# An attention and feed-forward kernel on one core: bits of the second head pair scaled in halves, four small transfers on ScalarE's queue, and several steps placed earlier in the order of units

## The chip, the cores and the metric

The kernel runs on one core of a Trainium2 chip. The metric is the device time of one execution in microseconds (us); the kernel before took 973.36 us, the median of 3 runs (972.34 to 974.44). A core has TensorE (PE, with its weight loads shown as PEld), VectorE (DVE), ScalarE (ACT), GpSimd (POOL) and SyncE (SP), which work side by side and wait for each other by semaphores. SP issues nearly all DMA transfers of this kernel.

## The reference

Four batches of 8 heads, 768 positions, head size 64, all in float32. The queries and keys of a head are put in 64 buckets by the signs of six projections, and a query sees only the keys of its own bucket. The result, 3072 tokens of 512 numbers, goes through a feed-forward layer.

```
q_bits = (q @ proj > 0);  k_bits = (k @ proj > 0)
mask   = bucket(q_bits) == bucket(k_bits)
scores = where(mask, q @ k.T / 8, -1e9);  attn = softmax(scores)
x = (attn @ v) as 3072 x 512
h = x @ w_in;   g = h if h >= 1, 0 if h <= -1, else (h + 1)^2 / 4
out = g @ w_out
```

## The kernel before

**Precision.** Products run in TensorE's fast float32 form (written F32R in the code, fp32r in the profile). Exactness comes from splitting an operand into a high and a low part: an exponential is held as `ph` plus `pl`, a value matrix as `va` plus `vb`, a weight as `hi` plus `lo`.

**Units.** The attention part goes over 32 heads in 16 pairs. A head has 12 units, numbered through as g: two halves of the queries (384 columns) by six blocks of 128 keys. I call g modulo 12 the place of a unit in its head. In unit g (the loop from L613) TensorE makes the scores of unit g (`s_unit`, two products, L369 and L370) into one of four PSUM buffers; ScalarE takes two exponentials of them (L378 `ph`, L383 in float32); and TensorE makes the three products of unit g - 4 with the values (`pv_unit`, L402, L404, L406). The low part `pl` (`lo_unit`, the subtraction of line 39) of unit g - 1 is made by DVE, or by POOL for key blocks 0 and 3.

**Rows of bits.** The mask is made by extra rows in the operand tiles T1 and T2: the bits of a pair are made by `bits_mm` (L208, then a comparison on DVE, L219), scaled (`bits_scale`) and put in place by four small transfers (`bits_put`, L280), one for each head h and each side t of the product.

**Maxima.** A score row needs its maximum over its bucket. `max_mm` (L308, two products into one PSUM tile `smax`) and `max_red` (L312, a reduction on DVE) do this for 128 queries at a time. There is one `smax` tile, so the next `max_mm` waits for the reduction before it. Which unit holds which maximum is written in the table `early` (L605 to L612): key 5g + 5 means the end of unit g, with the reduction put off until after the scores of unit g + 1; 5g + 2 means after `lo_unit`, with the reduction at once; 3 and 4 lie between the value products. From head 6 on a maximum stands at the end of units with places 4, 6, 8, 10, 0 and 2, and its reduction opens DVE's work of the next unit.

**Rows of maxima.** When the six maxima of a head are there, `max_clamp` limits them (two operations on POOL), `max_tr` turns them into a row by a transpose on TensorE (L347), and `max_put` copies the row from PSUM on ScalarE (L352) and sends it by DMA into T2 (L354) and into a flag row in HBM (L355). For head 2 this is done in two halves by `half_clamp` and `half_put` (L331, L333, L335). Heads 0 and 1 have their own way.

**Other work woven in.** `at(g, fn)` puts a step at the end of unit g, after the unit's own work on every engine; steps of one unit run in the order in which they were put. From head 3 on each head also carries one block of a weight matrix through a bit-level split (`WeightSplit.steps`): a load, a rescaling on ScalarE (L66), then on DVE the operations `tail` (L70), `shifted` (the shift-or, L74) and `signed` (L78), then rounding and subtraction. `conv` places these at offsets 0, 9, 10, 12, 14 and so on from a head's first unit, so `tail` ends the unit of place 10, `shifted` that of place 0 of the next head, and `signed` that of place 2. Their scratch lies in the PSUM bank `obank[0]`, which the value products of a head's first half need from place 4. For the first block, `signed` is at unit 50 and the products that need the bank start in unit 52. Three times, at the end of a batch, the softmax sums are loaded (`sums_load`, L667 and L668), combined on DVE (`sums_add`, L672 and L673) and inverted (`sums_inv`, L677); `sums_load` is at unit 104 for the first batch, `sums_add` 15 units later (place 11), `sums_inv` 21 units later (place 5).

**Feed-forward.** After the last unit, at about 456 us, the feed-forward part runs on TensorE without a gap to the end. The change touches none of it.

Of the kernel before, what the change touches and what calls it, by code (L numbers as in the profile page):

```python
# [11 lines left out]
F32 = mybir.dt.float32  # L12
F32R = mybir.dt.float32r
# [9 lines left out]
P = 128  # L23
NH = B * H
NPAIR = NH // 2
NJ = S // P
# [85 lines left out]
def attention(ctx, tc, wst, T1, T2, qk, v, pj, cv, x_d, s_d, e_d, tasks, shared):  # L112
# [15 lines left out]
    warm = const.tile([P, 2], F32, name="warm")  # L128
    nrow = [const.tile([P, NJ, 33], F32R, name=f"nrow{h}") for h in range(2)]
    pj_raw = const.tile([P, NB], F32, name="pj_raw")  # L130
    nmh = const.tile([P, 2, NJ], F32, name="nmh")
    pj_hi = const.tile([P, NB], F32R, name="pj_hi")
    pw = const.tile([P, 3, P], F32R, name="pw")
    VA = [const.tile([P, NJ, 3, D], F32R, name=f"va_{i}") for i in range(NV)]
# [128 lines left out]
        row_mm(hd, hf, ps)  # L263
        nc.scalar.copy(out=T2[0][32:33, 0, hd, hf * HS:(hf + 1) * HS], in_=ps[32:33, 0:HS])

    def bits_scale(pr, eng):
        bt, neg, _ = bits_t[pr]
        if eng is nc.scalar:
            eng.activation(out=bt, in_=neg, func=AF.Identity, scale=cvt[:, 0:1], bias=cvt[:, 1:2])
            return  # L270
        eng.tensor_scalar(out=bt, in0=neg, scalar1=cvt[:, 0:1], scalar2=cvt[:, 1:2],
                          op0=ALU.mult, op1=ALU.add)

    def bits_put(pr):
        t2 = T2[pr % NQK]
        bt, neg, _ = bits_t.pop(pr)
        for h in range(2):
            for t in range(2):
                i = 8 * (2 * t + h)
                nc.sync.dma_start(out=t2[0:8, t, h, :].bitcast(F32), in_=bt[i:i + 8, :].bitcast(F32))  # L280

    def load_v(pr):
        vraws[pr] = work.tile([P, NJ, 2, D], F32, name="vraw", bufs=1)
# [42 lines left out]
    def half_put(hd, hf, bank):  # L326
        pr, h = hd // 2, hd % 2
        if hf == 1:
            nms.pop(hd)
        ps = obank[bank]  # L330
        nc.tensor.transpose(out=ps[0:2 * HB, 0:P], in_=nmh[:, hf], identity=ident)  # L331
        te = small.tile([2 * NJ, P], F32R, name="te")[0:2 * HB]
        nc.scalar.copy(out=te, in_=ps[0:2 * HB, 0:P])  # L333
        sl = slice(hf * HS, (hf + 1) * HS)
        nc.sync.dma_start(out=T2[pr % NQK][7:8, 0, h, sl].bitcast(F32), in_=te[0:HB].bitcast(F32))  # L335
        nc.sync.dma_start(out=e_d[hd // H][hd % H:hd % H + 1, sl], in_=te[HB:2 * HB].bitcast(F32))

    def max_clamp(hd, eng):
        nm = nms[hd]
        eng.tensor_scalar(out=nm[:, NJ:2 * NJ], in0=nm[:, 0:NJ], scalar1=CLAMP, scalar2=None,  # L340
                          op0=ALU.is_gt)
        eng.tensor_scalar(out=nm[:, 0:NJ], in0=nm[:, 0:NJ], scalar1=CLAMP, scalar2=None,
                          op0=ALU.min)

    def max_tr(hd, bank=None):
        ps = mx[hd] = ps_s.tile([P, 512], F32, name="s") if bank is None else obank[bank]
        nc.tensor.transpose(out=ps[0:2 * NJ, 0:P], in_=nms.pop(hd), identity=ident)  # L347

    def max_put(hd):
        pr, h = hd // 2, hd % 2  # L350
        te = small.tile([2 * NJ, P], F32R, name="te")
        nc.scalar.copy(out=te, in_=mx.pop(hd)[0:2 * NJ, 0:P])  # L352
        if pr > 0:
            nc.sync.dma_start(out=T2[pr % NQK][7:8, 0, h, :].bitcast(F32), in_=te[0:NJ, :].bitcast(F32))  # L354
        nc.sync.dma_start(out=e_d[hd // H][hd % H:hd % H + 1, :], in_=te[NJ:2 * NJ, :].bitcast(F32))  # L355

    units = {}
# [96 lines left out]
    def at(g, fn, *a):  # L454
        tasks[g].append((fn, a))
# [90 lines left out]
    at(10, bits_mm, 1, 1, 0)  # L546
    at(10, split_v, 0, nc.gpsimd, 1)
    at(11, bits_cmp, 1, 1)
    at(11, bits_scale, 1, nc.scalar)
    at(12, bits_put, 1)  # L550
    at(12, move, 1, 2)
    at(12, max_tr, 0, 0)
    at(12, max_put, 0)
# [49 lines left out]
    NG = NH * NU  # L603
    red = None
    early = {}  # L605
    for hd, gs in ((0, (0, 2)), (1, (4, 5, 6, 8, 11, 12)), (2, (15, 16, 17, 19, 20, 22)), (3, (21, 23, 24, 26, 27, 29))):
        early.update({5 * n + 5: (hd, NJ - len(gs) + i) for i, n in enumerate(gs)})
    for i in range(2 * NJ):
        n = 5 * 31 + 35 * i // 4
        early[n + (n % 5 == 1)] = 4 + i // NJ, i % NJ  # L610
# [494 lines left out]
def lsh_attn_ffn(ctx: ExitStack, tc: tile.TileContext, qk, v, pj, cv, w_in, w_out, out):  # L1105
# [43 lines left out]
    def at(g, fn, *a):  # L1149
        tasks[g].append((fn, a))  # L1150

    def conv(g, steps, offs):
        for fn, n in zip(steps, offs):
            at(g + n, fn)
# [6 lines left out]
    def wi_steps(i, cp, stage=None):  # L1161
        return ws.steps(win_v[:, :, i * P:(i + 1) * P, :], (P, NCT, P, 2), wih[i], wil[i], cp, stage, None, wq[i], word)
# [4 lines left out]
    woh = [hi for hi, lo in wo]  # L1167
    wol = [lo for hi, lo in wo]
    for i in range(NW1):
        conv((2 * i + 3) * NU, wi_steps(i, nc.scalar), (0, 9, 10, 12, 14, 17, 19, 21))  # L1170
    g0 = (NH - 4) * NU
    late = {}
    for n in range(NSTG):
        i = n - (NFT - NW1)
        stage = wq[NW1 + n] if i < 0 else xdp.tile([P, DM], F32, name=f"wd{n}")
        if i < 0:
            first, late[n] = wi_steps(NW1 + n, nc.gpsimd, stage)
        elif i < 2:
            first, late[n] = wo_steps(i, nc.gpsimd, stage)
        else:  # L1180
            first, late[n] = wo_steps(i, nc.scalar, stage, nc.gpsimd if i < 4 else nc.vector)
        conv((4 + 2 * n) * NU, first, (0, 9, 10, 12, 14, 16))
    for n, g in enumerate((1, 7, 13, 25, 30, 35)):
        conv(g0 + g, late[n], (0, 5, 6))

# [1 line left out]
    for b in range(B - 1):  # L1187
        g = (b + 1) * H * NU + LAG + 4
        at(g, lambda b=b: xm.sums_load(*(attn["small"].tile([P, NF], F32, name=n, bufs=1) for n in ("sm", "em")), b))
        at(g + 15, xm.sums_add)  # L1190
        at(g + 21, xm.sums_inv, b)
    gx = (NH - 2) * NU

    def load_raw():
# [99 lines left out]
```

## Time and profile before

| | |
|---|---|
| median of 3 runs | 973.36 us (972.34 to 974.44) |
| the profiled execution | 974.55 us, of it 972.7 us from first to last instruction |
| PE busy (products) | 960.8 us, 99% |
| PEld busy (weight loads) | 890.6 us, 92% |
| DVE busy | 749.4 us, 77% |
| ACT busy | 680.4 us, 70% |
| POOL busy | 323.0 us, 33% |
| DMA, share of 16 engines | 59.6% on SP's queue |

A product's bar in the profile is longer than the step from one product to the next, because products are pipelined: one over 384 columns lasts 0.34 us, and the next starts some 0.175 us later. So lost time on PE is read from the starts of successive products and weight loads, and from the idle time in brackets at the end of a timeline row, which also names what ended it. The same holds for DVE and ACT, with a smaller overlap.

### The profile page before, as it was taken

The page shows a single profiled execution, that of the slowest core. Times are in us where ns is not written, and L with a number is a line of the kernel's source. Part 1 is how long each engine was busy: PE and PEld are TensorE (multiplying, and loading weights), DVE is VectorE, ACT ScalarE, POOL GpSimd, SP SyncE. Part 2 cuts the span into 40 slices and gives each one's busy share as a digit, 9 for nine tenths or more (in the row PEclk, how much of TensorE's full clock was granted, in tenths as well). Part 3 has the DMA queues.
Part 4 walks back from the last instruction along what each step waited for, and adds up shares of the span by engine and source line. Part 5 has one row for each costly group of instructions (what it writes and reads, how often), then busy time and mean ns, then how long its engine had stood idle before and what let it go on. Part 6 is the DMA issues. An engine that isn't in the chain of part 4 may idle for free.

```text
span 972.7 us, 15569 instructions
## 1 busy us (share of the span) xinstructions
PE 960.8 (99%) x5050; PEld 890.6 (92%) x5050; DVE 749.4 (77%) x1313; ACT 680.4 (70%) x1481; POOL 323.0 (33%) x433
## 2 busy tenths in 40 slices
PE   8999999999999999999999999999999999999998
PEld 7889999999999999999999998888998888888886
DVE  8778888988888888885987787787876777655554
ACT  7879998999999998988656565455464545544444
POOL 8767766666677766577000000000000000000000
PEclk9999999999999999999999999999999999999999
DMA  5776556567665566536592578976458554454431
GB/s 163 189 172 173 164 159 183 172 192 200 179 187 157 169 163 181 145 110 153 190 339 81 163 227 287 290 247 199 119 175 226 151 180 116 149 153 119 118 89 65
DMA packets 95112, 167.55 MB, mean 172 GB/s; under 512 B 13956, under 2 KB 51960, under 8 KB 95032
## 3 DMA queue, kind: packets, MB, share of 16 engines
q1 hardware_dynamic: 94808, 166.56, 59.6%
q8 instruction: 40, 0.66, 0.3%
q14 instruction: 40, 0.33, 0.1%
q10 hardware_dynamic: 224, 0.00, 0.0%
HBM read 106.13 MB, written 33.87 MB: 144 GB/s over the span
## 4 chain that ended last, share of the span: by engine, by line
PE 90%; DVE 3%; DMA 2%; ACT 2%; POOL 1%; issue 1%; SPq 1%; POOLq 0%; DVEq 0%; ACTq 0%
PE y L828 27%; PE h L1060 18%; PE h L965 7%; PE smax L308 7%; PE o L402 6%; PE o L406 6%; PE s L370 6%; PE o L404 6%; PE s L369 6%; PE o L208 2%; DVE nm L312 1%; DMA raw<-in_qk_dram 1%; DMA t<-bits 1%; DVE pl L39 1%; DMA t<-te 0%
## 5 line engine op out<-in xcount | busy, mean ns | idle before, releaser
L378 ACT ACTIVATE ph<-s 128x384 fp32r<-128x384 f32 x380 | 189.8, 499 | 38.8 <-PE s L370 32.3
L312 DVE TENSOR_REDUCE nm<-smax 128x1 f32<-128x768 f32 x189 | 180.0, 952 | 28.4 <-PE smax L308 28.2
L39 DVE TENSOR_TENSOR pl<-s,ph 128x384 fp32r<-128x384 f32 x256 | 138.1, 549 | 28.6 <-ACT s L383 24.1
L39 POOL TENSOR_TENSOR pl<-pf,ph 128x384 fp32r<-128x384 f32 x128 | 129.7, 1014 | 85.4 <-ACT pf L383 85.4
L793 DVE SCALAR_TENSOR_TENSOR t<-t 128x384 f32<-128x384 f32 x128 | 71.3, 557 | 106.5 <-ACT z L788 106.4
L369 PE MATMUL s<-t 128*128 128x384 f32 x384 | 131.2, 342 | 0.0
L370 PE MATMUL s<-t 128*128 128x384 f32 x384 | 129.6, 337 | 1.2 <-DMA t<-te 1.2
L402 PE MATMUL o<-ph,va 128*128 128x386 f32 x384 | 130.0, 339 | 0.4 <-DVE wsq L78 0.4
L404 PE MATMUL o<-ph,vb 128*128 128x386 f32 x384 | 130.0, 339 | 0.0
L406 PE MATMUL o<-pl,va 128*128 128x386 f32 x384 | 129.8, 338 | 0.0
L383 ACT ACTIVATE s<-s 128x384 f32<-128x384 f32 x252 | 126.3, 501 | 0.0
L828 PE MATMUL y<-t,ghi 128*128 128x512 f32 x384 | 124.6, 395 | 0.0
L308 PE MATMUL smax<-t 128*128 128x384 f32 x378 | 100.7, 347 | 3.6 <-DVE nm L312 3.0
L787 ACT ACTIVATE t<-h,mh 128x384 f32<-128x384 f32 x56 | 32.5, 581 | 83.5 <-PE h L965 43.8
L798 ACT CAST ghi<-z 128x384 fp32r<-128x384 f32 x129 | 65.1, 505 | 30.1 <-DVE z L794 26.4
L788 ACT ACTIVATE z<-t,m 128x384 f32<-128x384 f32 x128 | 79.0, 617 | 4.2
L828 PEld LDWEIGHTS y<-t,ghi 128*128 128x128 f32 x384 | 71.3, 188 | 11.1 <-ACT ghi L798 0.3
L1060 PE MATMUL h<-wbig,t 128*128 128x384 f32 x399 | 81.4, 336 | 0.0
L308 PEld LDWEIGHTS smax<-t 128*128 128x128 f32 x378 | 66.2, 188 | 14.9 <-DVE nm L312 13.6
L787 ACT ACTIVATE t<-wsq,mh 128x384 f32<-128x384 f32 x48 | 29.6, 617 | 67.0 <-DVE wsq L1073 40.7
L1060 PEld LDWEIGHTS h<-wbig,t 128*128 128x128 f32 x399 | 71.6, 188 | 5.3
L828 PE MATMUL y<-t,glo 128*128 128x512 f32 x192 | 76.0, 396 | 0.0
(192 smaller groups left out, 2072.9 us busy)
## 6 DMA issues: line engine op xcount, KB each, us to landing
t<-wc SPq DMA_DIRECT2D x92, 256.0 KB
t<-t SPq DMA_DIRECT2D x60, 384.0 KB
wraw<-wc SPq DMA_DIRECT2D x76, 256.0 KB
raw<-in_qk_dram SPq DMA_DIRECT2D x14, 768.0 KB
wraw<-in_w_in_dram SPq DMA_DIRECT2D x16, 512.0 KB
wraw<-in_w_out_dram SPq DMA_DIRECT2D x16, 512.0 KB
t<-ed SPq DMA_DIRECT2D x36, 192.0 KB
xd<-xs SPq DMA_DIRECT2D x32, 192.5 KB
```

Source lines behind the costliest of these rows:

```text
L39: eng.tensor_tensor(out=out, in0=a, in1=b, op=ALU.subtract)
L308: nc.tensor.matmul(out=smax[hd][:, hf, 0:HS], lhsT=t2[:, 0, h, i * P:(i + 1) * P], rhs=t2[:, 1, h, hf * HS:(hf + 1) * HS], start=True, sto ...
L312: nc.vector.tensor_reduce(out=nmp(hd)[:, i:i + 1], in_=smax[hd][:, :, 0:HS], axis=AX.XY, op=ALU.max, negate=True)
L369: nc.tensor.matmul(out=ps[:, 0:HS], lhsT=t1[:, 1, h, ks], rhs=t1[:, 0, h, sl], start=True, stop=False)
L370: nc.tensor.matmul(out=ps[:, 0:HS], lhsT=t2[:, 1, h, ks], rhs=t2[:, 0, h, sl], start=False, stop=True)
L378: nc.scalar.activation(out=ph[:, 0:HS], in_=ps[:, 0:HS], func=AF.Exp, scale=SCALE)
L383: nc.scalar.activation(out=pf, in_=ps[:, 0:HS], func=AF.Exp, scale=SCALE)
L402: nc.tensor.matmul(out=o, lhsT=wa, rhs=ph, start=(jj == 0), stop=False)
L404: nc.tensor.matmul(out=o, lhsT=wb, rhs=ph, start=False, stop=False)
L406: nc.tensor.matmul(out=o, lhsT=wa, rhs=pl, start=False, stop=(jj == NJ - 1))
L828: nc.tensor.matmul(out=ys[c][m], lhsT=g_[:, m * P:(m + 1) * P], rhs=w, start=(first and k == 0), stop=(last and k == 2))
L1060: nc.tensor.matmul(out=ps, lhsT=w[:, cs], rhs=x, start=(n == 0 and s not in (2, 3, 6)), stop=(n == 5), skip_group_check=True)
```

## The change

1. **Bits of pair 1.** `bits_scale(1)` on ScalarE, one operation over 768 columns at unit 11, becomes two over 384 columns, at units 10 and 11. `bits_put(1)` moves from unit 12 to unit 11, and one of its four transfers (head 0, side 1) is issued from ScalarE's queue instead of SP's.
2. **Rows by ScalarE's queue.** The row transfer of head 2's second half (`half_put`, hf = 1) and those of heads 3 and 4 (`max_put`) are issued from ScalarE's queue.
3. **Two maxima of head 1.** The table `early` is written with its keys in full; all are as before but two: 35 becomes 37 and 60 becomes 57.
4. **Row product.** For heads 2 to 31 the transpose (float32) becomes an ordinary product with the identity in F32R. `max_clamp` writes a new F32R tile `nmr` in place of `nm`, and `nmh` becomes F32R.
5. **Shift-or.** The offset of `shifted` goes from 12 to 11 for all blocks; `signed` of the first block goes from 14 to 13 (unit 49).
6. **Sums.** `sums_add` goes from 15 to 7 units after its reference unit (place 3), `sums_inv` from 21 to 19 (place 3 of the next head).

```diff
-    nmh = const.tile([P, 2, NJ], F32, name="nmh")
+    nmh = const.tile([P, 2, NJ], F32R, name="nmh")
...
-    def bits_scale(pr, eng):
+    def bits_scale(pr, eng, hf=None):
         bt, neg, _ = bits_t[pr]
+        if hf is not None:
+            bt, neg = (t[:, hf * HS:(hf + 1) * HS] for t in (bt, neg))
...
-                nc.sync.dma_start(out=t2[0:8, t, h, :].bitcast(F32), in_=bt[i:i + 8, :].bitcast(F32))
+                (nc.scalar if pr == 1 and h < t else nc.sync).dma_start(out=t2[0:8, t, h, :].bitcast(F32), in_=bt[i:i + 8, :].bitcast(F32))
...
-        nc.tensor.transpose(out=ps[0:2 * HB, 0:P], in_=nmh[:, hf], identity=ident)
+        nc.tensor.matmul(out=ps[0:2 * HB, 0:P], lhsT=nmh[:, hf], rhs=ident_r, start=True, stop=True)
...
-        nc.sync.dma_start(out=T2[pr % NQK][7:8, 0, h, sl].bitcast(F32), in_=te[0:HB].bitcast(F32))
+        (nc.sync if hf == 0 else nc.scalar).dma_start(out=T2[pr % NQK][7:8, 0, h, sl].bitcast(F32),
+                                                      in_=te[0:HB].bitcast(F32))
...
         nm = nms[hd]
-        eng.tensor_scalar(out=nm[:, NJ:2 * NJ], in0=nm[:, 0:NJ], scalar1=CLAMP, scalar2=None,
+        t = nms[hd] = small.tile([P, 2 * NJ], F32R, name="nmr")
+        eng.tensor_scalar(out=t[:, NJ:2 * NJ], in0=nm[:, 0:NJ], scalar1=CLAMP, scalar2=None,
                           op0=ALU.is_gt)
-        eng.tensor_scalar(out=nm[:, 0:NJ], in0=nm[:, 0:NJ], scalar1=CLAMP, scalar2=None,
+        eng.tensor_scalar(out=t[:, 0:NJ], in0=nm[:, 0:NJ], scalar1=CLAMP, scalar2=None,
                           op0=ALU.min)
...
-        nc.tensor.transpose(out=ps[0:2 * NJ, 0:P], in_=nms.pop(hd), identity=ident)
+        nm = nms.pop(hd)
+        if hd < 2:
+            nc.tensor.transpose(out=ps[0:2 * NJ, 0:P], in_=nm, identity=ident)
+        else:
+            nc.tensor.matmul(out=ps[0:2 * NJ, 0:P], lhsT=nm, rhs=ident_r, start=True, stop=True)
...
-            nc.sync.dma_start(out=T2[pr % NQK][7:8, 0, h, :].bitcast(F32), in_=te[0:NJ, :].bitcast(F32))
+            (nc.sync if hd > 4 else nc.scalar).dma_start(out=T2[pr % NQK][7:8, 0, h, :].bitcast(F32),
+                                                         in_=te[0:NJ, :].bitcast(F32))
...
-    at(11, bits_scale, 1, nc.scalar)
-    at(12, bits_put, 1)
+    at(10, bits_scale, 1, nc.scalar, 0)
+    at(11, bits_scale, 1, nc.scalar, 1)
+    at(11, bits_put, 1)
...
-    for hd, gs in ((0, (0, 2)), (1, (4, 5, 6, 8, 11, 12)), (2, (15, 16, 17, 19, 20, 22)), (3, (21, 23, 24, 26, 27, 29))):
-        early.update({5 * n + 5: (hd, NJ - len(gs) + i) for i, n in enumerate(gs)})
+    for hd, gs in ((0, (5, 15)), (1, (25, 30, 37, 45, 57, 65)), (2, (80, 85, 90, 100, 105, 115)),
+                   (3, (110, 120, 125, 135, 140, 150))):
+        early.update({n: (hd, NJ - len(gs) + i) for i, n in enumerate(gs)})
...
-        conv((2 * i + 3) * NU, wi_steps(i, nc.scalar), (0, 9, 10, 12, 14, 17, 19, 21))
+        conv((2 * i + 3) * NU, wi_steps(i, nc.scalar), (0, 9, 10, 11, 14 - (i == 0), 17, 19, 21))
...
-        conv((4 + 2 * n) * NU, first, (0, 9, 10, 12, 14, 16))
+        conv((4 + 2 * n) * NU, first, (0, 9, 10, 11, 14, 16))
...
-        at(g + 15, xm.sums_add)
-        at(g + 21, xm.sums_inv, b)
+        at(g + 7, xm.sums_add)
+        at(g + 19, xm.sums_inv, b)
```

## The prediction

> **What bounds the kernel now.** I read the cores' view first, then busy times, waits, and the timeline stretch by stretch.
>
> ```profile
> core 0: 972.7 us, clock 0.999
> ```
> ```profile
> PE 960.8 (99%) x5050; PEld 890.6 (92%) x5050; DVE 749.4 (77%) x1313; ACT 680.4 (70%) x1481; POOL 323.0 (33%) x433
> ```
>
> TensorE is the bound and its clock is full, so only two things can bring time: fewer product steps, or fewer gaps between them. Product bars overlap, so 99% hides gaps. They show in the waits of the products, and, from 84 to 400 us, in those of the weight loads:
>
> ```profile
> PE s L370 <- DMA t<-te: 1.2, 1, 1.2
> PE o L402 <- DVE wsq L78: 0.4, 1, 0.4
> ```
> ```profile
> PEld smax L308 <- DVE nm L312: 7.7, 23, 0.6
> ```
>
> The last row is the important one: once in each of 23 heads the load for a maximum waits for DVE's reduction, 7.7 us in all. One of them, first on PE, then on DVE:
>
> ```profile
> 93.92 0.19 PEld L404 LDWEIGHTS o<-ph,vb 128*128 128x128 f32 x1
> 94.10 0.19 PEld L406 LDWEIGHTS o<-pl,va 128*128 128x128 f32 x1
> 94.59 0.30 PEld L308 LDWEIGHTS smax<-t 128*128 128x128 f32 x2 [0.30 <-DVE nm L312]
> 94.88 0.19 PEld L369 LDWEIGHTS s<-t 128*128 128x128 f32 x1
> ```
> ```profile
> 90.34 0.69 DVE L70 TENSOR_SCALAR o<-wraw 128x512 int32<-128x512 int32 x1 [0.15 <-ACT xs L412]
> 90.94 0.95 DVE L312 TENSOR_REDUCE nm<-smax 128x1 f32<-128x768 f32 x1
> 91.81 1.21 DVE L39 TENSOR_TENSOR pl<-s,ph 128x384 fp32r<-128x384 f32 x2
> 92.94 0.74 DVE L74 SCALAR_TENSOR_TENSOR o<-wsq,wsc,o 128x512 int32<-128x512 int32 x1
> 93.59 0.95 DVE L312 TENSOR_REDUCE nm<-smax 128x1 f32<-128x768 f32 x1
> 94.46 0.55 DVE L39 TENSOR_TENSOR pl<-s,ph 128x384 fp32r<-128x384 f32 x1
> 94.92 0.74 DVE L78 SCALAR_TENSOR_TENSOR wsq<-wsq,wsc,o 128x512 int32<-128x512 int32 x1
> ```
>
> The steady step is 0.18 (93.92 to 94.10), so the load should start at 94.28; it starts at 94.59, when the reduction of 93.59 has ended. Behind it two loads fit in 0.29, one steady step and one of 0.11, so some 0.07 is caught up and 0.23 to 0.24 is lost. On DVE the shift-or (L74) stands directly ahead of the late reduction.
>
> **Shift-or and sums.** DVE's steps by starts: reduction 0.87 (90.94 to 91.81), shift-or 0.65, one low part 0.46 (94.46 to 94.92). Two low parts back to back would last 0.46 + 0.55 = 1.01, but took 1.21: DVE stood 0.20 between them, since the second needs this exponential, which ends at 92.43:
>
> ```profile
> 91.89 0.54 ACT L383 ACTIVATE s<-s 128x384 f32<-128x384 f32 x1
> ```
>
> At offset 11 the shift-or comes between those two low parts, and 0.20 of its 0.65 fills that hole. The sequence becomes 91.81 + 0.46 + 0.65 + 0.46 = 93.38 for the reduction, 0.21 earlier than 93.59. The load waits about 0.09 instead of 0.30, nearly all caught up. Gain 0.21 in each of 20 ordinary heads: 4.1 us. The ends are 0, if the hole belongs to DVE itself, and 0.24 x 20 = 4.8. The low part that is now behind the shift-or comes 0.45 later; its PSUM buffer and its product are wanted units later, so I cost that at nothing (0.45 a head if a unit had been waiting for it).
>
> The other three of the 23 hold the sums as well:
>
> ```profile
> 159.97 0.37 DVE L672 SCALAR_TENSOR_TENSOR sm<-em,sm 128x48 f32<-128x48 f32 x1
> 160.37 0.19 DVE L673 TENSOR_SCALAR sm<-sm 128x48 f32<-128x48 f32 x1
> ```
> ```profile
> 152.07 0.96 DVE L312 TENSOR_REDUCE nm<-smax 128x1 f32<-128x768 f32 x1 [0.37 <-PE smax L308]
> ```
> ```profile
> 143.38 0.59 SPq L145 DMA_DIRECT2D raw<-in_qk_dram  x1
> 144.07 1.30 SPq L667 DMA_DIRECT2D sm<-sd  x1
> 145.41 0.67 SPq L668 DMA_DIRECT2D em<-ed  x1
> ```
>
> There the wait is 0.6 (the longest of the 23), 0.53 lost, because the sums' half microsecond lies in the same place. At place 3 DVE has 0.37 idle before the reduction at 152.07, and that reduction's successor is not urgent. Gain 3 x 0.51 = 1.5; ends 0.9 and 1.6. It assumes that the loads have landed by 151.7, where DVE would now reach them. They sit in SP's queue behind a raw load issued at 143.38. The inversion, moved by two units, also falls in such a hole: nothing; its store passes SP's queue two units sooner, where nothing waits for it.
>
> **The first block** is different. Its wait (0.4 in the row of L78 above, some 0.55 with the restart) ends because `signed` moves to unit 49. But here a maximum stands inside unit 48:
>
> ```profile
> 78.07 0.95 DVE L312 TENSOR_REDUCE nm<-smax 128x1 f32<-128x768 f32 x1
> 78.94 0.75 DVE L74 SCALAR_TENSOR_TENSOR o<-wsq,wsc,o 128x512 int32<-128x512 int32 x1
> ```
>
> At unit 47 the shift-or comes ahead of this reduction, which then ends about 0.55 to 0.65 later, and the maximum of unit 50 waits for it. I take 0 (ends: 0.5 gained, 0.3 lost).
>
> **Rows by ScalarE's queue.** Head 3's row is the 1.2 us wait:
>
> ```profile
> 57.84 0.25 ACT L352 CAST te<-s 12x128 fp32r<-12x128 f32 x1 [0.47 <-PE s L347]
> ```
> ```profile
> 57.96 1.16 SPq L161 DMA_DIRECT2D t<-t  x2
> ```
> ```profile
> 59.21 4.35 DMA t<-te
> ```
>
> The row is ready at 58.09, SP issues two large moves first, then the row at 59.21, and it lands 4.35 later, at 63.56. The product could have run 1.2 earlier, at 62.3. On ScalarE's own queue it is issued at 58.1. The nearest row for a small transfer there stands at the kernel's start:
>
> ```profile
> 0.73 0.40 ACTq L461 DMA_DIRECT2D pj_raw<-in_pj_dram  x1
> ```
> ```profile
> 3.49 0.41 ACT L483 CAST pw<-pj_raw 64x6 fp32r<-64x6 f32 x2 [0.84 <-DMA pj_raw<-in_pj_dram]
> ```
>
> 2.8 us from issue to use, beside SP's first loads. So it lands near 61, before 62.3; at worst, as in SP's queue, 58.1 + 4.35 = 62.5. Gain 1.2 and the restart, 1.4 (ends 1.0 and 1.5, unless the queue makes no difference: a rival). The Trainium skill speaks against this: "DMA: Bandwidth & Descriptors", section "Issuing engines are not separate DMA queues", says that DMAs started by different engines run on the same 16 DMA engines and interleave, and that only issue time is saved. By it the row would still land with the moves; this trace cannot decide it, since both queues are busy only at its start.
>
> Head 4's row and head 2's second half show no wait in the table, so moving them brings nothing by itself; SP's queue is shorter by two issues, and nothing there is waited for. ScalarE pays for four issues, 0.4 (L461) to 0.74 each (the four pieces of 2.94 below), and the exponentials of units 12, 26, 33 and 44 stand behind them. Exponentials are used by products four units later, so three are covered; the one at unit 11 is counted next.
>
> **The early stretch.**
>
> ```profile
> 24.75 0.19 PEld L402 LDWEIGHTS o<-ph,va 128*128 128x128 f32 x1 [0.35 <-DVE neg L219]
> ```
> ```profile
> 28.54 0.62 PE L308 MATMUL smax<-t 128*128 128x384 f32 x2 [0.16 <-DVE nm L312]
> ```
> ```profile
> 27.75 1.01 ACT L269 ACTIVATE bits<-neg,cvt 32x768 fp32r<-32x768 f32 x1
> ```
> ```profile
> 28.83 2.94 SPq L280 DMA_DIRECT2D t<-bits  x4
> ```
>
> Key 37 fills a small wait at 20 us, but at 24.75 PE waits for a comparison whose place on DVE does not change, so that gain is lost again: 0. Key 57 puts its reduction earlier, and the wait at 28.54 goes (0.16 and restart: 0.3 to 0.4). It also puts 0.87 of reduction ahead of the comparison of pair 1's second half. So the halved scaling ends no earlier than now, near 28.8, and then ScalarE issues a transfer before the exponentials of unit 12: they come 0.5 to 0.9 late, and DVE's low parts with them, which takes back up to 0.4. On the other side the two pieces that head 2's first maximum needs (sides 0 and 1 of head 0) go out side by side instead of 0.74 apart, SP has one piece less, and the raw loads behind it, which feed POOL and head 3's row, come that much sooner. Net 0.5 (ends 0.3 lost, 1.0 gained).
>
> **Row product.** Thirty-one transposes become one-pass products. After a transpose and after the last of three F32R row products (L258) the next loads start:
>
> ```profile
> 98.05 0.19 PEld L369 LDWEIGHTS s<-t 128*128 128x128 f32 x1
> 98.16 0.19 PEld L370 LDWEIGHTS s<-t 128*128 128x128 f32 x1
> ```
> ```profile
> 30.96 0.19 PEld L369 LDWEIGHTS s<-t 128*128 128x128 f32 x1
> 31.07 0.19 PEld L370 LDWEIGHTS s<-t 128*128 128x128 f32 x1
> ```
>
> Both 0.11 apart: the load of the next 128 columns, not the short product, sets this step. I take 0 (ends 0 and half a step, 31 x 0.055 = 1.7). The clamps keep their number and shape.
>
> **Sum.** 4.1 + 1.5 + 0 + 1.4 + 0.5 + 0 = 7.5 us. The profiled execution took 974.55 (972.7 of span and 1.85 around it) and would take 967.05, a span of 965.2. It lies 1.19 above the median of 973.36, so the median forecast is 965.9. The feed-forward part from 456 us has no gaps of this kind and only moves.
>
> **Rivals.**
> *The row product is shorter after all.* For: a one-pass product streams half as long. Against: the equal 0.11 above. Another 1.7: 964.2. The skill's page "TensorE: Matmul & The Clock Gate", section "Wait — 56ns, not 53.3ns?", gives 55.6 ns for a warm 128-column step, which points this way; the trace's 0.11 after an F32R product does not agree.
> *ScalarE's queue does not help.* The row lands at 63.5 as before: 7.5 - 1.4 = 6.1 gained, 967.3.
> *DVE's hole does not fill* (the low part behind it still ends when it did, and the reduction with it): 4.1 falls away, 970.0. Against: DVE works in order and the shift-or's inputs are ready.
> *Eaten up:* the hole does not fill, and the four issues lie on the path with their full 0.4 to 0.74: 970.0 and 1.6 to 2.9 are 971.6 to 972.9, within 0.2% (1.95 us, about what a measurement of this kernel can tell from no change).
> *Slower: DVE waits for the sums' loads.* The nearest row for such a queue is the early raw load:
>
> ```profile
> 43.51 7.66 DMA raw<-in_qk_dram
> ```
>
> By it the raw load of 143.38 lands at 151.0 and the sums' loads just behind, against 151.7: 0.7 of margin. Were they to land at 154.9 or later, DVE would stand 3 us, at three places; 9 to 10 us lost, against 7.5 - 1.5 gained by the rest, gives 976 to 977. It turns slower than 975.3 when the loads take over about 9 us from their issue.
>
> **Chances.** Forecast 0.58 (own range 963.5 to 969, from the ends above and 1 us of scatter between runs); shorter row product 0.13; queue no help 0.10; hole not filled 0.07; eaten up 0.07; slower 0.05. So faster 0.88, within 0.2% 0.07, slower 0.05. The range 962.5 to 969.5 takes in the first three, 0.81.
>
> **What would show it.** Right: the loads of L308 between 84 and 400 us wait under 2.5 us in all; L370 no longer waits for `te`; L74 stands between two low parts; a wait of L308 on DVE appears near 79 us in place of L402's. Wrong: reductions of place 1 no earlier against PE, DVE idle before L672, the next loads after L347's successor less than 0.11 apart, or ScalarE's gaps after its issues ending in waits of PE.

## The result and the profile after

The changed kernel takes 968.82 us, the median of 6 runs (968.37 to 969.17), against 973.90 of the kernel before in 6 runs of the same series (972.34 to 975.70). The ratio is 0.9948, with a 95% interval of 0.9936 to 0.9959: about 5.1 us less, where 7.5 were forecast. The profiled execution took 968.67, of it 966.7 of span, 6.0 less than before.

The cores' view and the busy times of the page after show the same bound, with a full clock:

```profile
core 0: 966.7 us, clock 0.999
```
```profile
PE 956.6 (99%) x5050; PEld 889.8 (92%) x5050; DVE 747.8 (77%) x1313; ACT 680.4 (70%) x1482; POOL 322.4 (33%) x433
```

The counts of products and loads are unchanged, so the time came out of the gaps. The waits of weight loads between 84 and 400 us, whose row of before was 7.7 us in 23 places:

```profile
PEld s L355 <- POOL nmr L346: 1.1, 7, 0.2
PEld smax L310 <- DVE nm L314: 0.7, 3, 0.4
```

The view leaves out waits under 0.15 us: by the starts of the loads, the load for the maximum still waits 0.07 to 0.13 in most heads, near the 0.09 that was forecast. The row of GpSimd's clamp (L346), for which the row product waits, is new; it comes back under "Shift-or and sums alone".

The largest waits of products over the whole span. The product no longer waits for the DMA of head 3's row (`t<-te`, 1.2 before); the wait of the row product L258 for ScalarE's copy `te` is new:

```profile
PE smax L310 <- DVE nm L314: 2.0, 8, 0.4
PE smax L432 <- DVE idle L477: 1.3, 1, 1.3
PE o L258 <- ACT te L360: 0.9, 1, 0.9
```

To see where the gain falls I lay the two traces side by side by unit: the start of the first score product of each unit (L369 before, L378 after) in TensorE's timeline, and the difference.

| stretch | after minus before, us |
|---|---|
| start, to unit 5 | +0.21 |
| units 5 to 36 | +0.28 |
| unit 36 to 37 (head 3's row) | -1.51 |
| units 37 to 60 (first block) | -0.01 |
| units 60 to 330 (shift-or and sums) | -4.95 |
| units 330 to the last, 383 | -0.07 |
| all | -6.05 |

Unit 5 differs by up to 0.58 us from before between the profiles shown below, whatever was changed, so the first row is scatter.

**The hole is filled.** VectorE after, on the stretch that the prediction worked out, and the load that follows:

```profile
89.98 0.95 DVE L314 TENSOR_REDUCE nm<-smax 128x1 f32<-128x768 f32 x1
90.84 0.55 DVE L39 TENSOR_TENSOR pl<-s,ph 128x384 fp32r<-128x384 f32 x1
91.31 0.75 DVE L74 SCALAR_TENSOR_TENSOR o<-wsq,wsc,o 128x512 int32<-128x512 int32 x1
91.96 0.55 DVE L39 TENSOR_TENSOR pl<-s,ph 128x384 fp32r<-128x384 f32 x1
92.43 0.95 DVE L314 TENSOR_REDUCE nm<-smax 128x1 f32<-128x768 f32 x1
```
```profile
93.43 0.30 PEld L310 LDWEIGHTS smax<-t 128*128 128x128 f32 x2 [0.17 <-DVE nm L314]
```

From one reduction to the next it is 2.45 us (89.98 to 92.43); before it was 2.65 (90.94 to 93.59). The shift-or stands between the low parts and the 0.20 of idle time is gone.

**The early loss.** ScalarE after, around the two halves of the scaling, and the product of TensorE that waits:

```profile
28.67 0.71 ACT L271 ACTIVATE bits<-neg,cvt 32x384 fp32r<-32x384 f32 x1 [0.17 <-DVE neg L219]
29.45 0.79 ACTq L282 DMA_DIRECT2D t<-bits  x1
30.61 0.49 ACT L387 ACTIVATE ph<-s 128x384 fp32r<-128x384 f32 x1 [1.24 <-PE s L379]
31.00 0.49 ACT L392 ACTIVATE pf<-s 128x384 f32<-128x384 f32 x1
31.37 0.24 ACT L360 CAST te<-o 12x128 fp32r<-12x128 f32 x1
```
```profile
31.66 0.37 PE L258 MATMUL o<-ident_r,nrow 128*33 128x128 f32 x3 [0.86 <-ACT te L360]
```

Before, the copy `te` of head 0's row ran at 29.40:

```profile
29.40 0.24 ACT L352 CAST te<-o 12x128 fp32r<-12x128 f32 x1
```

It now stands behind the second half of the scaling, the issue and two exponentials, at 31.37, and the row product (in the same PSUM bank) waits 0.86 for it. Unit 15 starts 0.85 late, where unit 13 had been 0.20 early. Of that, 0.2 and 0.4 come back at units 28 and 33.

**The first block** lost its wait at L411 and got the one expected near 79 us:

```profile
78.64 0.62 PE L310 MATMUL smax<-t 128*128 128x384 f32 x2 [0.41 <-DVE nm L314]
```

### The profile page after: what moved, and what is told of

Its sections match the earlier page's. It is cut to its first block, busy times and chain, and to the rows that moved or that the text cites. A ratio compares the mean times of both kernels' runs of the same rounds, so it can differ in the third digit from the quotient of the medians.

```text
span 966.7 us, 15568 instructions
## 1 busy us (share of the span) xinstructions
PE 956.6 (99%) x5050; PEld 889.8 (92%) x5050; DVE 747.8 (77%) x1313; ACT 680.4 (70%) x1482; POOL 322.4 (33%) x433
## 4 chain that ended last, share of the span: by engine, by line
PE 94%; DVE 2%; ACT 1%; issue 0%; ACTq 0%; DVEq 0%
PE y L839 27%; PE h L1071 18%; PE h L976 7%; PE smax L310 7%; PE o L411 7%; PE o L415 7%; PE s L378 7%; PE o L413 7%; PE s L379 6%; PE o L208 2%; DVE nm L314 1%; ACT ph L387 0%; ACT t L798 0%; ACT z L799 0%; PE s L355 0%
## 5 line engine op out<-in xcount | busy, mean ns | idle before, releaser
L39 DVE TENSOR_TENSOR pl<-s,ph 128x384 fp32r<-128x384 f32 x256 | 137.5, 548 | 28.8 <-ACT s L392 27.8
L378 PE MATMUL s<-t 128*128 128x384 f32 x384 | 130.5, 340 | 0.0
L411 PE MATMUL o<-ph,va 128*128 128x386 f32 x384 | 130.1, 339 | 0.2 <-DVE neg L219 0.2
L839 PE MATMUL y<-woh,glo 128*128 128x512 f32 x192 | 75.7, 394 | 0.2
```

The source lines that it names most:

```text
L39: eng.tensor_tensor(out=out, in0=a, in1=b, op=ALU.subtract)
L378: nc.tensor.matmul(out=ps[:, 0:HS], lhsT=t1[:, 1, h, ks], rhs=t1[:, 0, h, sl], start=True, stop=False)
L411: nc.tensor.matmul(out=o, lhsT=wa, rhs=ph, start=(jj == 0), stop=False)
L839: nc.tensor.matmul(out=ys[c][m], lhsT=g_[:, m * P:(m + 1) * P], rhs=w, start=(first and k == 0), stop=(last and k == 2))
```

## The experiments

Times are medians. The kernel before varied from series to series (972.82, 973.90, 975.04, 975.23 and 975.26), and the series behind the variants ran on four chips. So variants of the changed kernel are compared by their own medians and, where it matters, by unit starts.

**Shift-or and sums alone.** The kernel before with parts 5 and 6 and nothing else.

```diff
-        conv((2 * i + 3) * NU, wi_steps(i, nc.scalar), (0, 9, 10, 12, 14, 17, 19, 21))
+        conv((2 * i + 3) * NU, wi_steps(i, nc.scalar), (0, 9, 10, 11, 14 - (i == 0), 17, 19, 21))
...
-        at(g + 15, xm.sums_add)
-        at(g + 21, xm.sums_inv, b)
+        at(g + 7, xm.sums_add)
+        at(g + 19, xm.sums_inv, b)
```

> The kernel before with only the shift-or at offset 11 (first block: signed at 13) and the sums at 7 and 19. Theory (the shift-or's place is the gain): 4.6 to 5.2 us faster than before, all of it between units 60 and 330, with head 1 to 3 as before: the 1.2 us wait for head 3's row stays, and the first block trades one wait for another (0, within 0.2). Rival (it needs the other parts): under 3 us.

969.93 us, ratio 0.9948 [0.9930, 0.9966]. Units 60 to 330 take 4.45 less than before, against 4.95 in the changed kernel: these two parts carry nearly all of that stretch, a little less than the 4.6 expected at least. The row wait is still there, and head 2's half row (needed at unit 31) has one too:

```profile
PE s L370 <- DMA t<-te: 2.1, 2, 1.2
```

Where the missing half microsecond lies can be read from the traces. Every second head gains only 0.03 to 0.09 here, against 0.17 to 0.21 in the changed kernel (with the sums 0.37 to 0.39 against 0.50 to 0.52); the other heads take part of it back. In those 11 heads the load of the row product waits for GpSimd's second clamp. The wait in this run, then the two clamps of one head in this run and in the changed kernel:

```profile
PEld s L347 <- POOL nm L342: 3.3, 11, 0.3
```
```profile
137.78 0.25 POOL L340 TENSOR_SCALAR nm<-nm 128x6 f32<-128x6 f32 x1
138.11 0.23 POOL L342 TENSOR_SCALAR nm<-nm 128x6 f32<-128x6 f32 x1
```
```profile
136.21 0.24 POOL L344 TENSOR_SCALAR nmr<-nm 128x6 fp32r<-128x6 f32 x1
136.41 0.24 POOL L346 TENSOR_SCALAR nmr<-nm 128x6 fp32r<-128x6 f32 x1
```

Where both clamps write into the tile `nm` that they read, the second starts 0.33 after the first; into the new tile `nmr` of part 4 it starts 0.20 after it, and the wait is 0.14 to 0.18 instead of 0.28 to 0.32. The one-pass product is not the reason: with transposes and this tile ("Transposes" below) the wait is 0.14 to 0.20. Before, it was at most 0.09 in the same heads, since TensorE came later. So part of what VectorE gave was taken back by the next engine in line, and the clamps' own tile, which had been counted at nothing, seems to have returned some of that. No run moves this tile alone.

**Sums back.** The changed kernel with the sums at 15 and 21.

```diff
-        at(g + 7, xm.sums_add)
-        at(g + 19, xm.sums_inv, b)
+        at(g + 15, xm.sums_add)
+        at(g + 21, xm.sums_inv, b)
```

> The changed kernel with the sums' add and reciprocal back at 15 and 21 units after their loads. The prediction's theory (the add of 0.93 us stood on VectorE where two shift-ors of a head meet it, and made TensorE wait 0.5 us at each of three places) expects three waits of the maxima for VectorE of about 0.5 us each, near 150, 300 and 530 us, and a span about 1.5 us longer than the changed kernel's. Rival: once the shift-or is a unit earlier the old place of the add hits free time as well, and moving it was worth nothing; then the span is the changed kernel's to 0.3 us.

969.29 us, span 967.4: 0.5 to 0.7 more, between the two theories. Unit starts say why. A head with the sums gains 0.50 in the changed kernel and 0.17 to 0.19 here, which is what any head gains from the shift-or. So the sums' move is worth 0.33 at each of three places, 1.0 us. The places are at 158.8, 267.0 and 375.2 us, not at the 150, 300 and 530 named above. The first one in this run, on VectorE and on the loads:

```profile
158.77 0.20 DVE L683 SCALAR_TENSOR_TENSOR sm<-em,sm 128x48 f32<-128x48 f32 x1
159.01 0.19 DVE L684 TENSOR_SCALAR sm<-sm 128x48 f32<-128x48 f32 x1
159.11 0.55 DVE L39 TENSOR_TENSOR pl<-s,ph 128x384 fp32r<-128x384 f32 x1
```
```profile
160.58 0.30 PEld L310 LDWEIGHTS smax<-t 128*128 128x128 f32 x2 [0.41 <-DVE nm L314]
```

The changed kernel did not get the whole 1.0, because at the second of its places VectorE waits for the sums' load, and TensorE for VectorE:

```profile
258.25 0.66 DVE L683 SCALAR_TENSOR_TENSOR sm<-em,sm 128x48 f32<-128x48 f32 x1 [0.43 <-DMA em<-ed]
```
```profile
260.05 0.30 PEld L310 LDWEIGHTS smax<-t 128*128 128x128 f32 x2 [0.37 <-DVE nm L314]
```

Units 210 to 216 lose 0.27 there. This is the mechanism of the rival on the slower side, at one place in three and a tenth of its size. It too is a draw: of the eleven profiles with the sums at their new place, four lose time there and seven do not.

**Shift-or at offset 10.** The changed kernel with every shift-or but the first block's one unit earlier still.

```diff
-        conv((2 * i + 3) * NU, wi_steps(i, nc.scalar), (0, 9, 10, 11, 14 - (i == 0), 17, 19, 21))
+        conv((2 * i + 3) * NU, wi_steps(i, nc.scalar), (0, 9, 10, 10 + (i == 0), 14 - (i == 0), 17, 19, 21))
...
-        conv((4 + 2 * n) * NU, first, (0, 9, 10, 11, 14, 16))
+        conv((4 + 2 * n) * NU, first, (0, 9, 10, 10, 14, 16))
```

> The changed kernel with every shift-or but the first block's one unit earlier still, at offset 10 instead of 11. The prediction's theory (the gain is a hole: VectorE stood free between two reductions of the maxima at offset 11, and at offset 12 it did not) says that the place matters, not the distance from offset 12: at 10 the 0.95 us shift-or and the 0.55 us copy meet a reduction again, TensorE waits 0.2 to 0.4 us for it in each of some 20 heads, and the time is 4 to 7 us longer than the changed kernel's, which gives the gain back. Rival: the gain came only from taking the shift-or away from the last reduction of a head; then 10 does as well as 11, and the span is the changed kernel's to 0.5 us.

980.31 us, ratio 1.0070 [1.0052, 1.0088]: slower than the kernel before. Against the changed kernel some 0.50 is lost in each of 23 heads between units 60 and 330, against the kernel before 0.29 on average. The place decides, not the distance; the loss is about twice what I expected. (The shift-or lasts 0.76 us; the 0.95 named above is a reduction's.) VectorE, and the product that waits:

```profile
89.29 0.70 DVE L70 TENSOR_SCALAR o<-wraw 128x512 int32<-128x512 int32 x1
90.09 0.76 DVE L74 SCALAR_TENSOR_TENSOR o<-wsq,wsc,o 128x512 int32<-128x512 int32 x1
90.75 0.95 DVE L314 TENSOR_REDUCE nm<-smax 128x1 f32<-128x768 f32 x1
91.62 1.01 DVE L39 TENSOR_TENSOR pl<-s,ph 128x384 fp32r<-128x384 f32 x2
```
```profile
91.76 0.62 PE L310 MATMUL smax<-t 128*128 128x384 f32 x2 [0.36 <-DVE nm L314]
```

Here `tail` and the shift-or stand together ahead of a reduction that in the changed kernel started at 89.98 and now starts at 90.75. At offset 12 one maximum came 0.23 late; here one comes late by 0.36 of product wait and its restart. The two low parts in a row (1.01, no idle) show that the hole has gone unused because VectorE is late, not because anything fills it.

**First block back to 12.** The changed kernel with the first block's shift-or at its old place.

```diff
-        conv((2 * i + 3) * NU, wi_steps(i, nc.scalar), (0, 9, 10, 11, 14 - (i == 0), 17, 19, 21))
+        conv((2 * i + 3) * NU, wi_steps(i, nc.scalar), (0, 9, 10, 11 + (i == 0), 14 - (i == 0), 17, 19, 21))
```

> The changed kernel with the first block's shift-or at its old offset 12 (its signing stays at 13). The prediction's theory (in the first block the earlier shift-or only trades a wait of the value product for a wait of the maxima near 78.6 us) expects the 0.41 us wait of the maxima there to go, a wait of a value product for VectorE not to come back because the signing is a unit earlier, and a gain of 0 to 0.6 us, 0.5 if both are gone. Rival: the wait at that place is of VectorE's sum of work, whatever its order; then one of the two waits is there with 0.4 to 0.6 us and the time is the changed kernel's.

968.65 us. Between units 48 and 60 it gains 0.26 on the changed kernel; the product wait near 79 us is gone and L411's did not come back. So the first block would have had about a quarter of a microsecond with `signed` alone moved; the early shift-or cancelled it. The profiled execution shows none of this in its span (967.4), as head 2's half row came late there, at unit 31:

```profile
PE s L379 <- DMA t<-te: 1.3, 1, 1.3
```

**Transposes.** The changed kernel with the float32 transposes in place of the one-pass products.

```diff
...
-            nc.tensor.matmul(out=ps[0:2 * NJ, 0:P], lhsT=nm, rhs=ident_r, start=True, stop=True)
+            nc.tensor.transpose(out=ps[0:2 * NJ, 0:P], in_=nm, identity=ident)
```

The clamps keep their own tile `nmr`, now in float32, so this run is about the products alone.

> The changed kernel with the 31 row products as float32 transposes again. Theory (the next load of 128 columns sets the step): same time within 0.3 us, and the next two loads 0.11 us apart in both. Rival (one pass is half as long): 1.7 us slower, 0.055 us at each of 31 places.

969.10 us against 968.82, spans 966.9 and 966.7: no difference beyond scatter. The loads behind the row product, in this run and in the changed kernel:

```profile
97.01 0.09 PEld L355 LDWEIGHTS s<-ident,nmr 128*12 128x12 f32 x1
97.19 0.19 PEld L378 LDWEIGHTS s<-t 128*128 128x128 f32 x1
97.30 0.19 PEld L379 LDWEIGHTS s<-t 128*128 128x128 f32 x1
```
```profile
96.71 0.09 PEld L355 LDWEIGHTS s<-ident_r,nmr 128*12 128x12 f32 x1
96.89 0.19 PEld L378 LDWEIGHTS s<-t 128*128 128x128 f32 x1
97.00 0.19 PEld L379 LDWEIGHTS s<-t 128*128 128x128 f32 x1
```

Both 0.18 and 0.11 apart: the next load of 128 columns sets the step. The bar of the product itself did get shorter, from a mean of 273 ns to 224, and brought nothing. The page "TensorE: Matmul & The Clock Gate" of the Trainium skill gives 55.6 ns from one warm 128-column product to the next, in its section "Wait — 56ns, not 53.3ns?"; behind this product the trace has 0.11 us from load to load, and the measurement decides.

**Key 60.** The changed kernel with the maximum at 57 back at 60.

```diff
-    for hd, gs in ((0, (5, 15)), (1, (25, 30, 37, 45, 57, 65)), (2, (80, 85, 90, 100, 105, 115)),
+    for hd, gs in ((0, (5, 15)), (1, (25, 30, 37, 45, 60, 65)), (2, (80, 85, 90, 100, 105, 115)),
```

> The changed kernel with one of head 1's maxima back from place 57 to 60. If the place was what held TensorE's wait at 28.5 us away, as the prediction has it, that wait of 0.3 to 0.4 us comes back and unit 13 starts that much later. A second theory: the maximum at 57 keeps VectorE from the comparison of the second pair's bits, so ScalarE's scaling starts late and the copy of head 0's row with it; then the row product's wait of 0.86 us near 31 us shrinks by 0.2 to 0.6, and the sum is within 0.3 us of the changed kernel's either way. If neither, unit 15 starts as in the changed kernel.

968.48 us. Both expectations came: the wait at 28.5 is back and the row product's has shrunk from 0.86 to 0.17.

```profile
28.47 0.62 PE L310 MATMUL smax<-t 128*128 128x384 f32 x2 [0.18 <-DVE nm L314]
31.10 0.37 PE L258 MATMUL o<-ident_r,nrow 128*33 128x128 f32 x3 [0.17 <-ACT te L360]
```

From unit 12 to 17 it gains 0.27 on the changed kernel: key 57 costs 0.27 net, since its reduction of 0.96 stands ahead of the comparison that the scaling waits for.

**Bits by SP.** The changed kernel with the one piece of bits issued by SP again.

```diff
-                (nc.scalar if pr == 1 and h < t else nc.sync).dma_start(out=t2[0:8, t, h, :].bitcast(F32), in_=bt[i:i + 8, :].bitcast(F32))
+                nc.sync.dma_start(out=t2[0:8, t, h, :].bitcast(F32), in_=bt[i:i + 8, :].bitcast(F32))
```

> The changed kernel with the one bits piece back on SP's queue (still in halves, at unit 11); rows stay on ScalarE's. Theory (ScalarE's 0.79 us issue holds up the copy of head 0's row, for which the row product of unit 14 waits 0.86 us): that wait falls under 0.3 us and unit 15 starts 0.6 to 0.9 us earlier than in the changed kernel; but head 2's first maximum then waits up to 0.9 us for the second piece, and the raw loads behind SP's queue come up to 0.7 us later, so that head 3's row may be late by up to 0.7 us. Sum: -0.3 to +0.7 us against the changed kernel. Rival (the wait has another cause, the halves themselves): the 0.86 us wait stays.

968.79 us, no difference (0.18 less by unit starts between units 5 and 36). Without the 0.79 issue on ScalarE the wait of L258 is gone, and head 2's first maximum waits for the piece instead:

```profile
PE smax L310 <- DMA t<-bits: 0.7, 1, 0.7
```

**Rows by SP.** The changed kernel with its three row transfers on SP's queue.

```diff
...
-            (nc.sync if hd > 4 else nc.scalar).dma_start(out=T2[pr % NQK][7:8, 0, h, :].bitcast(F32),
-                                                         in_=te[0:NJ, :].bitcast(F32))
+            nc.sync.dma_start(out=T2[pr % NQK][7:8, 0, h, :].bitcast(F32), in_=te[0:NJ, :].bitcast(F32))
```

> The changed kernel with the three row transfers (head 2's second half, heads 3 and 4) back on SP's queue; the bits piece stays on ScalarE's. Theory of the prediction (ScalarE's queue brings head 3's row past the moves): the product of unit 36 waits 1.2 to 1.5 us again, total 1.2 to 1.5 us slower than the changed kernel. Rival (the row rides in with the large moves on the same engines, and came in time because those moves were issued 1.2 us earlier): no wait over 0.3 us at unit 36, total within 0.4 us of the changed kernel.

968.19 us, and no wait for `te`. Taken by itself this says that ScalarE's queue did nothing. But in this run the two large moves were issued early, at 56.67 as against 57.96 before, so SP was free for the row:

```profile
56.67 1.16 SPq L161 DMA_DIRECT2D t<-t  x2
58.29 0.84 SPq L362 DMA_DIRECT2D t<-te  x1
```

The moves wait for casts on GpSimd, and these for a raw load. Its issue lies at 42.8 to 44.5 us in all profiles, its landing anywhere from 48.5 to 51.7. So the question needed two runs with the moves at the same time.

**Late moves, by either queue.** A memset on GpSimd ahead of the casts, written three times, holds them until about 51.6 us; the row goes by ScalarE's queue in the first kernel, by SP's in the second.

```diff
     for h, g in enumerate((20, 2 * NU + 1)):
-        at(g, lambda h=h: nc.gpsimd.memset(T2[0][32:33, 0, h].bitcast(F32), 0.0))
+        for _ in range(1 + 2 * h):
+            at(g, lambda h=h: nc.gpsimd.memset(T2[0][32:33, 0, h].bitcast(F32), 0.0))
```

> The changed kernel with a memset of 0.73 us on GpSimd written three times instead of once ahead of the casts of the fourth pair (the same zeros), so that these start no earlier than about 51.6 us whenever the raw load has landed, and the two large moves are issued at about 58.2 and 58.8 us, as in the kernel before. Head 3's row goes by ScalarE's queue. Theory A (that queue gets the row in ahead of the moves when these are late): the row is issued at about 58.4, lands before the second move, and the score product has no wait for it; the span is the changed kernel's to 0.4 us. Rival B (the row rides behind the moves whatever issues it, and the runs without a wait had early moves): the wait of 1.0 to 1.6 us is back here too.

> The same late moves with the three row transfers by SP's queue. Theory A: the row is issued only behind the two moves, at about 59.5 us, lands behind them at about 63.8, and the score product waits 1.0 to 1.6 us for it, as in the kernel before; the span is 1.0 to 1.6 us longer than the run with ScalarE's queue. Rival B: the same wait in both runs and no difference. A third case, no wait in either, would say that late moves were not the cause of the wait.

968.66 us by ScalarE's queue (4 runs, 968.28 to 970.11) and 969.56 by SP's (5 runs, 969.48 to 970.15). Unit 37 starts 1.53 us apart. The issues, first with ScalarE's queue (one row each of SP and ScalarE), then with SP's:

```profile
58.09 1.16 SPq L161 DMA_DIRECT2D t<-t  x2
```
```profile
58.21 0.75 ACTq L362 DMA_DIRECT2D t<-te  x1
```
```profile
58.27 1.16 SPq L161 DMA_DIRECT2D t<-t  x2
59.52 1.20 SPq L362 DMA_DIRECT2D t<-te  x1
```

By SP the row takes its turn behind both moves, and the score product waits for it as in the kernel before:

```profile
63.92 0.44 PE L379 MATMUL s<-t 128*128 128x384 f32 x1 [1.24 <-DMA t<-te]
```

By the trace's records of DMA ends the row landed at 62.02 in the first run, between the two moves (61.83 and 63.61), and at 63.88 in the second, just behind them (63.77). So the product waits 1.2 us for the row where SP issues it behind late moves, and in no other case; "moves" is the issue of the first of the two:

| kernel | moves | row issued | product wait for head 3's row |
|---|---|---|---|
| before | 57.96 | SP 59.21 | 1.2 |
| shift-or and sums alone | 58.52 | SP 59.77 | 1.2 |
| rows by SP | 56.67 | SP 58.29 | none |
| late moves, SP | 58.27 | SP 59.52 | 1.2 |
| after | 56.72 | ScalarE 58.41 | none |
| transposes | 57.87 | ScalarE 58.69 | none |
| sums back | 58.16 | ScalarE 58.42 | none |
| late moves, ScalarE | 58.09 | ScalarE 58.21 | none |

The six profiles left out go by ScalarE's queue, with moves from 56.19 to 58.32; four have no wait there, two one of 0.3 to 0.4 on the load (rows issued at 58.24 and 59.38).

ScalarE's queue has a price, too. The issue, 0.75 at 58.41 in the changed kernel, stands ahead of ScalarE's operation that feeds a comparison of bits (L214), and TensorE then waits for that comparison:

```profile
60.32 0.19 PEld L411 LDWEIGHTS o<-ph,va 128*128 128x128 f32 x1 [0.23 <-DVE neg L219]
```

All ten profiles with the row on ScalarE's queue have this wait, and the step to unit 35 is 0.15 to 0.21 longer there; the four by SP have neither.

**Rows alone.** The kernel before with part 2 alone (the edit of `half_put` and `max_put` in the diff above).

```diff
...
-            nc.sync.dma_start(out=T2[pr % NQK][7:8, 0, h, :].bitcast(F32), in_=te[0:NJ, :].bitcast(F32))
+            (nc.sync if hd > 4 else nc.scalar).dma_start(out=T2[pr % NQK][7:8, 0, h, :].bitcast(F32),
+                                                         in_=te[0:NJ, :].bitcast(F32))
```

> The kernel before with one part of the change alone: the second half of head 2's row and the rows of heads 3 and 4 go by ScalarE's queue. The times of the kernel before fall into two groups, 972.5 to 973.2 and 974.5 to 975.8. Theory A (the wait of the score product for head 3's row, 1.2 to 1.6 us, is there when the moves are late, and ScalarE's queue takes it away) expects no wait for the row in the profile, and times that stay with the lower group, 971.5 to 973.2, for most executions. Rival B (ScalarE's queue does not help in itself, or its issue of 0.75 us holds up ScalarE's exponentials as much): the wait is there in the profile or the time still falls into the two groups. If the wait is gone and the upper group is still there, the groups have another cause, and that stays open.

973.49 us (11 runs, 973.12 to 974.62) against 975.04 (15 runs, 972.79 to 976.10), ratio 0.9989 [0.9980, 0.9998]. Head 3's row no longer makes anything wait: unit 37 starts 0.88 early where unit 36 was 0.63 late, 1.51 together, with the moves at 58.32. Of 15 runs of the kernel before 12 took 974.3 or more, of these 11 only three did. The times did not come down to 973.2 as a whole; in the profiled execution (974.06) head 2's half row, also on ScalarE's queue, was late at unit 31:

```profile
54.68 0.45 PE L372 MATMUL s<-t 128*128 128x384 f32 x1 [1.20 <-DMA t<-te]
```

**Key 60 and first block together.** The changed kernel with both of these edits.

> The changed kernel with head 1's maximum back at place 60 and the first block's shift-or back at offset 12: what the two single runs showed in unit starts is 0.26 us less for each, with ScalarE's queue and the halves kept. Expected, if the two add up: a span 0.3 to 0.8 us below the changed kernel's, a median of 967.9 to 968.6. If they don't, the sum of work in front of unit 60 is what counts and the median stays at 968.6 to 969.0.

968.57 us, 6 runs, 967.96 to 969.30, against 968.82. Unit starts show both gains (0.28 and 0.25), and the profile loses 0.31 to a row that landed a little late at unit 37. The median lies where expected; the span, 966.5, is only 0.2 below the changed kernel's, short of the 0.3 to 0.8 expected. A quarter of a microsecond is within the scatter of these runs: not a measurable improvement.

## Why the prediction was right, and where it was wrong

The sign and the size hold: 968.8 lies inside 962.5 to 969.5, near its upper end, 2.9 above the forecast. Two of the signs of being wrong showed in a small way: VectorE idle ahead of the sums at one place (0.43), and a gap of ScalarE behind an issue that ended in a wait of TensorE (0.86).

**Shift-or.** The mechanism was right, and its place was tested from both sides: at 11 it gains, at 10 it loses more than at 12. The term was 4.1 (20 x 0.21 is 4.2); units 60 to 330 gained 4.95, of which three heads with sums had 0.50 each and one place lost 0.27, so the other 20 had 3.7, or 0.19 each. But with shift-or and sums alone these 20 had 3.3, or 0.165 each: in every second head the row product then waited 0.3 for GpSimd's clamp, a wait that the prediction did not look for. Some 0.4 of the 3.7 came with the rest of the change, and the traces point to the clamps' own tile. That the term came so near its 4.1 is in part luck.

**Sums.** 1.5 was right in gross (3 x 0.50) and 0.27 too high in net, since the second load landed after VectorE had got there. With shift-or and sums alone the three heads had 0.38 each, for the same reason as above. The prediction had 0.7 us of margin from one raw load's duration, and priced only a wait long enough to turn the sign.

**First block.** Right: one wait for the other, 0. It was not seen that `signed` alone would have brought 0.26.

**Rows.** The effect was right (1.51, forecast 1.4) and the reason holds, with a price and a condition. The price: the prediction held that the exponentials behind the issues were covered, and did not look at the operation for the comparison, which cost 0.17 at unit 35. The condition: ScalarE's queue is worth this where the moves are late. In the profile of the changed kernel they were early, and there SP's queue would probably have done as well, as it did in "Rows by SP" with moves at 56.67. The sentence from the Trainium skill ("DMA: Bandwidth & Descriptors", section "Issuing engines are not separate DMA queues") agrees with the runs in what it says: issued 1.1 behind the second move, the row from ScalarE's queue landed just behind it (62.49 after 62.31 in the changed kernel), and what was saved was the time of issue, 58.21 against 59.52. What I drew from it, that the row would still land with the moves, was wrong when the row could be issued ahead of the second one. Nor is the order of issue a rule: with the transposes the row was issued 0.26 behind the second move and landed 0.87 ahead of it (62.61 and 63.48), with the shift-or at offset 10 it was 0.44 behind and 0.86 ahead (62.06 and 62.92). By SP it was issued 0.69 behind and landed 0.11 behind (63.88 and 63.77, late moves). Whether the queue or the shorter distance makes this difference is not shown.

**Early stretch.** This step failed: 0.5 gained was forecast, 0.28 lost was measured between units 5 and 36, the lower end; 0.17 of this is the price of head 3's row at unit 35, so this step itself lost 0.11. "So the halved scaling ends no earlier than now, near 28.8" was off by 0.6 (it ended at 29.38; 0.2 of this was there from the first units on). The second half could start only when its comparison was done, at 28.63 against 27.51 before, since key 57's reduction now stood ahead of it, and it then lasted 0.71, where half of the whole's 1.01 would be 0.5. The step also named only exponentials behind the issue. The work that mattered behind it was the copy `te` of head 0's row, which frees a PSUM bank for TensorE. "Key 57 ... the wait at 28.54 goes" was right and did not pay: it cost 0.27 net, since it delays the comparison. "Key 37 ... that gain is lost again" was right.

**Row product.** Right for the product: 0. That "the clamps keep their number and shape" did not make them cost the same: in a tile of their own they end 0.11 sooner (by the starts, 0.20 apart instead of 0.31), which counts once the shift-or has moved.

**From the profiled execution to the median.** This step failed too. I took 1.19 off because the profiled execution of before lay that far above its median. But it was an execution with the row wait, which the change removes, so part of that distance was counted twice; the profiled execution of the changed kernel lies 0.15 below its median. Of the 2.9 us, 1.2 + 0.15 are this step; the rest is 0.6 of the early stretch, 0.2 of the row's price, 0.4 of the shift-or, 0.3 of the sums and 0.2 of scatter at the start, less 0.1 that the row's wait gave above the forecast.

What stays open: the times of the kernel before lie in two groups, 972.3 to 973.4 and 974.3 to 976.1. One row wait of 1.5 or two of 2.7 in all would make such groups, and moving the rows thinned out the upper one, but no execution of the lower group was profiled. Also open is why head 2's half row was late in three profiles, once by SP's queue and twice by ScalarE's. And no run separates the clamps' own tile from the rest of the change.

## What to carry to other kernels

An operation in an engine's order is worth what stands idle at its place: moved by one unit it filled a hole and gained 0.19 a head, by one more it lost 0.50 against that. The gain ends where the next engine is late, here GpSimd's clamps, so look at the waits behind the one that goes. Before a step is put on another engine's queue, list all that stands behind it there, first of all the copies that free a buffer and whatever feeds another engine. And a wait for a DMA in one profile is one draw: look at the spread of times, and hold the other transfers still, before a queue is given the credit.

## What was not expected of the hardware

Halving an activation of 32 x 768 into two of 32 x 384 cost 0.69 + 0.71 against 1.01 us; by my estimate from these three some 0.4 of each does not depend on the length. A DMA issue on ScalarE held it 0.69 to 0.82 us. Two small operations on GpSimd (128 x 6) started 0.31 to 0.33 us apart when both wrote into the tile that they read, and 0.20 when they wrote to another. The same raw load, issued within 1.7 us, took between 5.5 and 8.1 us to land in different executions (43.05 to 48.51 and 43.43 to 51.49).
